# Loading the first experts' weights in half pieces beside the attention, on one Trainium2 core

## The chip, the cores and the metric

The kernel runs on one core of one Trainium2 chip. The time is the device time of one execution in microseconds (us). A kernel is executed several times, in turns with the kernel before on the same chip. An execution is called fast or slow by its time against the fastest of the same kernel, and ratios use fast executions alone. TensorE is written PE, its weight loads PEld, VectorE DVE, ScalarE ACT, GpSimd POOL and SyncE SP.

## The reference, cut to what matters

A recurrent attention (4 batches, 8 heads, 768 steps, head width 48) makes 3072 rows of 384. A router deals these rows out to 8 experts, 384 rows each, and each expert is two matrix products with a ReLU between.

```python
for t in range(S):                                      # attention, per batch and head
    cur = einsum(u * k[t], v[t])
    y[t] = einsum(r[t], state + cur)
    state = w[t][:, None] * state + einsum(k[t], v[t])
# x = the rows of y, 3072 x 384
logits = x @ w_gate                                     # 8 experts
order = argsort(-logits.flatten())                      # a row goes to its best expert that has room
...                                                     # (cut) cap = 384 rows for each expert
for e in range(8):
    out[mask_e] = maximum(x[mask_e] @ w1[e], 0) @ w2[e] # w1: 384 x 1024, w2: 1024 x 384
```

## The kernel before

The attention is cut into 24 units (6 pieces of 128 steps for each of 4 batches). Each unit needs four loads of 192 KB, of r, k, v and w, which SyncE issues on a hardware queue. Some units later come the logits; the routing starts on the first rows ("early") while the last units are still at work, so that the experts can begin soon after unit 23. A scheduler in the program orders all instructions by planned times; `op["G", 16]` below is unit 16's step G, the score products, and `after=[...]` makes an instruction follow others in the plan.

The experts' weights (768 KB as bf16 for each of w1 and w2) are loaded by GpSimd, because they are f32 in memory and become bf16 on the way. The first four experts have buffers of their own; the other four reuse the attention's buffers.

```python
def _weight_loads(nc, e, w1sb, w2sb, moe_w1, moe_w2):
    return [lambda: nc.gpsimd.dma_start(
                out=w1sb, in_=moe_w1[e].rearrange("(fc p) f -> p fc f", p=128)),
            lambda: nc.gpsimd.dma_start(
                out=w2sb, in_=moe_w2[e].rearrange("(fc p) d -> p fc d", p=128))]

LOADS = 16
# ... (cut) inside the planning of the whole program:
for e in range(E):
    users = []                                   # (cut) steps that must be over before reuse, e >= 4
    both = []
    for i, fn in enumerate(_weight_loads(nc, e, *weights[e], moe_w1, moe_w2)):
        by = [op["G", LOADS + 2 * len(loads)]] if len(loads) < 3 else []
        a = line.add("Wi", (e, i), "POOL", 800, fn, after=begun + users + by, prio=-0.9)
        begun = [a] if not loads else [a, loads[-1]]
        loads.append(line.add("Wd", (e, i), "DMA", 3500, lambda: None, after=[a],
                              lag=1900, prio=-0.3))
        both.append(loads[-1])
    loaded.append(both)
```

So the first three loads are planned beside units 16, 18 and 20, and every later one follows when the one before is planned to have landed. How far ahead the attention's own loads are issued is set by a table:

```python
PACE = {"Lw": [("G", 5)], "Lk": [("T1", 3)], "Lr": [("U", 3)], "Lv": [("T0", 1)]}
```

## Time and profile before

| | before |
|---|---|
| time, median of 3 executions | 253.95 us (252.87 to 258.76) |
| time of the execution that was profiled | 266.54 us, its span 264.6 us |
| PE busy in that span | 215.1 us (81%), mean granted clock 0.931 |
| DMA packets | 118388, mean 160 GB/s |
| weight loads | 16 of 768 KB, by GpSimd |
| attention loads | 96 of 192 KB, by SyncE |

The profiled execution took 12.6 us more than the median one. The prediction below shows the lines of this profile and reads them.

### The profile page before, as it was taken

Reading aid. Unit: us, or ns where it says so; the run is one execution under the profiler, and the core shown is the slowest. Engines: PE = TensorE matmul, PEld = TensorE weight load, DVE = VectorE, ACT = ScalarE, POOL = GpSimd, SP = SyncE. Lnnn points to the kernel's source line nnn. Section 1 sums busy time; section 2 is a strip of 40 time slices with the busy share of each in tenths; the row PEclk is TensorE's granted clock in tenths of the full one; section 3 lists DMA queues with packets and bytes.
Section 4 is the critical chain, followed back from the end, with each engine's and each line's share of the span. In section 5 each row is a group of like instructions: output and inputs, shape, how many; then the busy total and the mean of one; then the engine's idle time right before and its main releaser. Section 6 shows DMA issues by size and latency. Waiting matters only on the chain.

```text
span 264.6 us, 10437 instructions
## 1 busy us (share of the span) xinstructions
PE 215.1 (81%) x4469; PEld 160.1 (61%) x4469; DVE 142.9 (54%) x440; ACT 131.3 (50%) x248; POOL 148.6 (56%) x180
## 2 busy tenths in 40 slices
PE   2189998799999799789689491899899997959980
PEld 0166776577777587656477370777566765736850
DVE  6757667385677566557268760274755660114450
ACT  2156776485777577457344320374755663402300
POOL 7435685555766558747634548157764647563341
PEclk9999999999999999999779855699999999997995
DMA  7978789488879768999996993979999999231111
GB/s 149 183 148 165 143 168 223 92 173 194 160 152 214 143 131 172 193 197 168 177 228 95 206 175 80 180 165 221 167 198 213 201 191 266 86 112 67 59 69 62
DMA packets 118388, 42.24 MB, mean 160 GB/s; under 512 B 101440, under 2 KB 113728, under 8 KB 118336
## 3 DMA queue, kind: packets, MB, share of 16 engines
q1 hardware_dynamic: 104128, 21.84, 41.0%
q0 software_dynamic: 14208, 19.66, 38.3%
q8 instruction: 37, 0.61, 0.9%
q14 instruction: 15, 0.12, 0.2%
HBM read 46.61 MB, written 7.47 MB: 204 GB/s over the span
## 4 chain that ended last, share of the span: by engine, by line
PE 68%; DVE 8%; DMA 8%; issue 7%; another core or an unknown queue 3%; ACT 3%; POOL 2%; POOLq 0%; DVEq 0%
PE yps L320 11%; PE tps L478 8%; PE gps L320 7%; PE tps L320 7%; PE cps L320 7%; PE gps L1117 6%; PE gps L1148 6%; PE cps L1117 6%; PE cps L1148 5%; DMA vv<-in_moe_w_dram 4%; DMA ww<-in_w_dram 3%; PE tps L590 2%; PE tps L1087 1%; DVE Dohl L870 1%
## 5 line engine op out<-in xcount | busy, mean ns | idle before, releaser
L466 POOL TENSOR_TENSOR mm<-diag,dd 128x512 f32<-128x512 f32 x24 | 25.1, 1048 | 57.5 <-DVE dd L461 31.1
L484 ACT COPY krT<-tps 112x512 f32<-112x512 f32 x48 | 28.1, 586 | 23.4 <-PE tps L478 20.4
L1168 POOL DMA_INDIRECT out_dram<-Fos,tok x24 | 24.1, 1003 | 24.7 <-DVE Fos L1158 13.7
L1076 POOL DMA_INDIRECT Fxg<-x_scratch,tok x24 | 23.5, 977 | 20.3 <-PE tps L1087 11.1
L557 DVE COPY_PREDICATED mm<-mask,gps 128x256 f32<-128x256 uint8 x48 | 18.7, 442 | 27.9 <-PE gps L320 16.7
L320 PE MATMUL cps<-ww,negut 128*128 128x384 f32 x48 | 23.3, 569 | 12.1 <-issue 6.3
L478 PE MATMUL tps<-ident,krs 128*112 128x128 f32 x192 | 31.5, 290 | 0.6 <-DVE Dboth L710 0.6
L478 PEld LDWEIGHTS tps<-ident,krs 128*112 128x112 f32 x192 | 22.7, 140 | 10.9 <-issue 6.2
L320 PE MATMUL yps<-mm,vv 64*48 64x64 f32 x768 | 19.9, 232 | 9.0 <-DVE mm L557 6.0
L457 POOL TENSOR_TENSOR rku<-rku,u_bc 128x384 f32<-128x384 f32 x24 | 24.0, 1000 | 2.6 <-DMA u_bc<-in_u_dram 2.6
L453 POOL TENSOR_TENSOR rku<-kr 128x384 f32<-128x384 f32 x24 | 24.1, 1003 | 2.2 <-DMA kr<-in_r_dram 2.2
L320 PEld LDWEIGHTS yps<-mm,vv 64*48 64x48 f32 x768 | 14.6, 125 | 17.5 <-DVE mm L557 10.7
L1148 PEld LDWEIGHTS <-Fhs 128*128 128x128 bf16 x192 | 17.8, 99 | 11.9 <-issue 2.8
L578 ACT COPY xf<-yps 128x512 f32<-128x512 f32 x24 | 14.0, 582 | 22.1 <-PE yps L320 22.1
L447 DVE TENSOR_TENSOR krs<-kr,cps 128x768 f32<-128x768 f32 x24 | 22.7, 945 | 1.7 <-ACT cps L442 1.6
L320 PE MATMUL yps<-krT,sm 48*48 48x64 f32 x384 | 21.6, 229 | 1.1 <-issue 1.1
L442 ACT ACTIVATE cps<-cps 128x768 f32<-128x768 f32 x24 | 19.3, 804 | 5.0 <-DVE cps L438 5.0
L320 PE MATMUL yps<-krT,st 48*48 48x64 f32 x384 | 21.3, 228 | 0.3 <-issue 0.3
L1134 ACT ACTIVATE Fhs<-gps 128x512 bf16<-128x512 f32 x20 | 12.0, 598 | 15.5 <-PE gps L1117 9.4
L320 PE MATMUL gps<-krT 48*64 48x64 f32 x768 | 18.4, 227 | 1.0 <-issue 1.0
L1134 ACT ACTIVATE Fhs<-cps 128x512 bf16<-128x512 f32 x20 | 11.8, 598 | 13.8 <-PE cps L1117 10.3
L1117 PEld LDWEIGHTS <-w 128*128 128x128 bf16 x192 | 15.1, 100 | 5.8 <-issue 4.1
(200 smaller groups left out, 464.5 us busy)
## 6 DMA issues: line engine op xcount, KB each, us to landing
w<-in_moe_w_dram POOLq DMA_DIRECT2D x8, 768.0 KB
ww<-in_w_dram SPq DMA_DIRECT2D x24, 192.0 KB, 3.9
kr<-in_k_dram SPq DMA_DIRECT2D x24, 192.0 KB, 4.0
kr<-in_r_dram SPq DMA_DIRECT2D x24, 192.0 KB, 4.2
vv<-in_v_dram SPq DMA_DIRECT2D x24, 192.0 KB, 4.1
kr<-in_moe_w_dram POOLq DMA_DIRECT2D x4, 768.0 KB
x_scratch<-row SPq DMA_DIRECT2D x7, 384.0 KB, 4.9
vv<-in_moe_w_dram POOLq DMA_DIRECT2D x2, 768.0 KB
```

Source lines behind the costliest of these rows:

```text
L320: ln.last = nc.tensor.matmul(*a, **kw)
L447: fn=lambda u=u, kr=kr, b=b: nc.vector.tensor_tensor(out=KR[slot(("kr", u))][:, :, :, :D], in0=kr[:, b].rearrange("t x (h d) -> t x h d", ...
L453: fn=lambda u=u, kr=kr, b=b: nc.gpsimd.tensor_tensor(out=P[slot(("p", u))], in0=kr[:, b, 0, :], in1=kr[:, b, 1, :], op=ALU.mult))
L457: fn=lambda u=u: nc.gpsimd.tensor_tensor(out=P[slot(("p", u))], in0=P[slot(("p", u))], in1=u_bc, op=ALU.mult))
L466: fn=lambda u=u: nc.gpsimd.tensor_tensor(out=M[slot(("m", u))], in0=_free(diag, [0, 2], [0, NPAIR], [1, 64]), in1=_free(Dg[slot(("dg", u)) ...
L478: ln.last = nc.tensor.transpose(t[:112, at:at + 128], pair_of(s[:, x], j), ident)
L484: nc.scalar.copy(out=KRT[slot(("krt", u))][:112, 2 * half:2 * half + 2].rearrange("p j x t -> p (j x t)"), in_=Tps[slot(("t", u, half))][: ...
L1076: got = nc.gpsimd.indirect_dma_start(out=self.xg[slot[xg[1]]], out_offset=None, in_=self.x_dram, in_offset=bass.IndirectOffsetOnAxis(ap=to ...
L1117: nc.tensor.matmul(self.bank("B", b[1])[:, i * size:(i + 1) * size], lhsT=w1sb[:, k, f8 * 128:(f8 + 1) * 128], rhs=xv()[:, k], start=(k == ...
L1134: nc.scalar.activation(out=to, in_=of, func=AF.Relu)
L1148: nc.tensor.matmul(self.bank("B", b[1])[:, :DX], lhsT=hv()[:, f8, h * 128:(h + 1) * 128], rhs=w2sb[:, f8, :], start=(f8 == 0), stop=(f8 == ...
L1168: put = nc.gpsimd.indirect_dma_start(out=self.out, out_offset=bass.IndirectOffsetOnAxis(ap=tok[:, j:j + 1], axis=0), in_=self.os[slot[o[1] ...
```

## The change

The intent was to take the weight loads away from the last units of the attention, where the routing, the attention's own end and the hand-over to the experts meet. The loads of the first four experts are cut into 16 half pieces of 384 KB, planned one beside each of units 5 to 20. None stands beside units 21 to 23. The loads of the last four experts are halved too, and start behind the last unit.

```diff
-    return [lambda: nc.gpsimd.dma_start(
-                out=w1sb, in_=moe_w1[e].rearrange("(fc p) f -> p fc f", p=128)),
-            lambda: nc.gpsimd.dma_start(
-                out=w2sb, in_=moe_w2[e].rearrange("(fc p) d -> p fc d", p=128))]
+    w1 = moe_w1[e].rearrange("(fc p) f -> p fc f", p=128)
+    w2 = moe_w2[e].rearrange("(fc p) d -> p fc d", p=128)
+    f, k = F // 2, F // 256
+    return [lambda to=to, of=of: nc.gpsimd.dma_start(out=to, in_=of)
+            for to, of in ((w1sb[:, :, :f], w1[:, :, :f]), (w1sb[:, :, f:], w1[:, :, f:]),
+                           (w2sb[:, :k], w2[:, :k]), (w2sb[:, k:], w2[:, k:]))]
@@
-LOADS = 16
+LOADS = 5
@@
-                by = [op["G", LOADS + 2 * len(loads)]] if len(loads) < 3 else []
+                n = len(loads)
+                by = [op["G", LOADS + n if n < 4 * OWN else last]]
                 a = line.add("Wi", (e, i), "POOL", 800, fn, after=begun + users + by, prio=-0.9)
-                begun = [a] if not loads else [a, loads[-1]]
-                loads.append(line.add("Wd", (e, i), "DMA", 3500, lambda: None, after=[a],
+                begun = [a] if n < 4 * OWN else [a, loads[n - 2]]
+                loads.append(line.add("Wd", (e, i), "DMA", 1750, lambda: None, after=[a],
                                       lag=1900, prio=-0.3))
-                both.append(loads[-1])
+                both += [loads[-1]] * (i % 2)
```

## The prediction

> **What bounds the kernel now.** I read the page's forty slices first, then the busy table by stretches, then the chain that ended last in order of time, then the timelines of GpSimd and of TensorE around the gaps in it, and last the packets of the transfers. The stretches are: the quiet part of the attention (units 8 to 15), the last units with the weight loads beside them, the hand-over, and the experts.
>
> ```profile
> 60.00:100.00 40.00, 37.97 (x1123) 29.10 (x1126) 25.73 (x63) 26.73 (x52) 25.22 (x30) 1.00 0.81 166
> 112.00:130.00 18.00, 13.72 (x434) 10.42 (x425) 9.68 (x23) 10.63 (x20) 11.10 (x13) 0.98 1.04 186
> 130.00:140.00 10.00, 9.12 (x181) 6.70 (x181) 5.90 (x15) 4.30 (x10) 4.32 (x5) 0.70 0.99 187
> 140.00:158.00 18.00, 13.55 (x364) 10.94 (x363) 13.95 (x55) 6.39 (x12) 7.64 (x10) 0.77 1.01 167
> 158.00:171.00 13.00, 6.67 (x109) 4.84 (x107) 1.03 (x3) 2.25 (x6) 6.67 (x8) 0.53 0.66 124
> 171.00:208.00 37.00, 35.86 (x299) 25.66 (x300) 21.46 (x96) 21.68 (x43) 23.13 (x25) 1.00 1.00 197
> ```
>
> The columns are the stretch, its length, busy time of PE, PEld, DVE, ACT and POOL, the granted clock, the DMA share and GB/s. In the quiet part PE is busy 37.97 of 40 us and the DMA 0.81 of it: PE bounds, but the DMA has only a fifth left. From 112 to 158 the DMA is full, PE falls to 36.4 of 46 us, and the clock sinks. From 171 the experts keep PE at 97% again.
>
> The chain says what those gaps are:
>
> ```profile
> 118.97 1.05 SPq L333 DMA_DIRECT2D vv<-in_v_dram  x1
> ...
> 119.36 0.95 POOL L1026 DMA_DIRECT2D w<-in_moe_w_dram  x1
> ...
> 120.13 8.59 DMA ww<-in_w_dram
> 128.74 0.85 ACT ww L399
> 129.63 1.65 PE cps L320 x2
> ...
> 157.21 7.93 another core or an unknown queue
> ...
> 208.45 11.26 DMA vv<-in_moe_w_dram
> 219.76 1.48 PE gps L1117 x12
> ```
>
> A whole weight load (768 KB) is triggered at 119.36; the attention's own load of w, issued at 120.13, lands 8.59 us later where the median of these loads is 3.9, and the next matmul runs at half clock (1.65 us, against 0.71 in the quiet part). The second gap lies between the scores of the last unit and their use. The third is less than it looks: the timeline of PE shows it at work during most of those 11.26 us,
>
> ```profile
> 219.76 1.48 PE L1117 MATMUL gps<-Fxe,vv 128*128 128x256 bf16 x12 [1.65 <-DMA vv<-in_moe_w_dram]
> ```
>
> so that the late weights of the last expert cost 1.65 us.
>
> As a clock for the units I take the starts of their score matmuls (gps<-krT) in PE's timeline: unit 5 at 43.5, 16 at 104.2, 21 at 141.1, 23 at 157.4; the first expert matmul comes at 171.4. Units 5 to 16 take (104.2-43.5)/11 = 5.5 us each, units 16 to 23 take 53.2/7 = 7.6.
>
> **What the Trainium skill says.** "DMA: Bandwidth & Descriptors", section "Queues, rings and completion order": each of the 16 engines takes turns between its queues packet by packet. The trace agrees, to the loads' harm: in the packet records the attention's packets are 192 B and those of w1 2048 B, and while the first w1 load drains, 17 to 24 KB of the former go per 1.5 us beside 256 to 274 KB of the latter, some 8%, near 192/(192+2048). A drain of a whole load, about 5 us, is thus nearly a stop for the attention's loads. "Runtime: NRT & Kernel Launch", section "Instruction fetch mechanics": instructions come in 16 KiB blocks by the same DMA. The records show such blocks 4.6 us apart on average in the quiet part and 6 to 10 us apart around the five drains from 108 to 158: PE's waits marked "issue" belong to this. "TensorE: Matmul & The Clock Gate", section "What's actually happening": idle time of some microseconds halves the clock; the 0.53 from 158 to 171 agrees.
>
> **The change, part by part.** Bytes stay the same. Sixteen halves of 384 KB, planned beside units 5 to 20, replace eight whole loads, of which six are now triggered from 104.90 to 147.93 and two at 163.68 and 164.48, behind the first gathers. The other four experts' loads are halved too; they move ahead of where they are, since the first experts' loads are no longer in front of them. In the order of instructions, PE's list is unchanged up to the end of the last unit, where the first gathered rows now stand ahead of two small transposes; GpSimd gets its triggers between the attention's products, and none in the last units before the gathers.
>
> Removed, in times of this trace. (a) Units 16 to 23 take 53.2 us where 7 x 5.5 = 38.5 would be quiet; 14.7 over. Of this some 4 is the early routing, which stays (PE waited 3.46 us for VectorE at 151.2, with no load in it): 10.5 removed. (b) From the last scores to the first expert matmul are 14.0 us. Its own work, summed from the timeline's rows at full clock: scores 0.6, masks 0.8, products 1, two evictions 1.2, transposes 0.9, one wait for gather and eviction 2, is 6.5; 7.5 is removable. But the 7.93 of it is charged to an unknown queue, not to a weight transfer, and the profiled execution (266.5 us) is itself 12.5 over the median timed one, so it may not be there in timed runs. I count 5. (c) The wait for the last expert's weights: 1.65. Sum 17.
>
> Added. (d) DMA work per unit from the fastest rates in the packet records: 4096 packets of 192 B at 1600 per 1.5 us are 3.84 us; a quarter of a 384 KB store is 0.45; half a weight load is 384 packets of w1 at 156 per 1.5 us halved, 1.85, or 512 of w2 at 400 per 1.5 us, 1.92. Sum 6.2 us, against the 5.5 the unit takes now: the DMA becomes the bound of units 5 to 20. 16 x (6.2-5.5) = 11. (e) Triggers: whole ones take 818 and 944 ns; eight more before and eight more after the hand-over, at some 0.85 us, are 7 us of GpSimd each time. A unit occupies it 1.00+1.00+1.05+0.5 = 3.6 us of 5.5, and in the experts it is busy 23.1 of 37 us, so this fits beside: 0.
>
> Net 17-11 = 6 us, 2.4% of 254: 248.
>
> **The rivals.** First, the spread costs more than it removes. For it: where both kinds of transfer were in flight the DMA moved 186 GB/s at a share of 1; a unit with half a load needs 786+98+393 = 1277 KB, so 6.9 us at that rate, and 16 x 1.4 = 22 us are added instead of 11; then the time is 259. Against it: that rate includes stalls of the issuing queues behind a whole load, and the experts' stretch reaches 197 to 218 GB/s. Second, the halves disappear in the idle fifth of the DMA: a half stops the attention's loads for only 2 us, less than the slack of most of them (k, r and v are issued several us before use; only w has about 1). Then (d) is 3 to 4 us and the time is 240. Third, the end does not move because it hangs on the routing: the first gather waits for the early routing, which follows unit 19's logits by a long chain on VectorE. In the trace the row numbers are ready at 156.0, only 1.3 us before the last scores; if units 20 to 23 speed up, this chain takes the wait's place. It caps (a)+(b) at perhaps 10 and makes 251 to 254. A fourth, that the experts wait for weights 4 to 7, I think unlikely: their triggers come some 12 us earlier.
>
> **Range and chances.** The middle of the working is 248; the second rival reaches 240, the first and third 251 to 259. I take 241 to 255 for 8 in 10. Gain over 2% means below 248.9, just above the middle: 0.52. Within 2% 0.39. Slower than 259 needs the first rival in full: 0.09.
>
> **What would show it.** Right: the chain no longer holds a wait of 8 us for ww; the DMA share from unit 5 to 20 is 0.95 or more instead of 0.81, and those units take 6.0 to 6.4 us each; unit 23's scores start between 150 and 160, the first expert matmul 6 to 8 us later; PE has no wait for vv in the experts; the granted clock stays at 1.00 through 130 to 140. Wrong: units 5 to 20 take near 5.5 us (second rival) or near 7 (first); or PE stands before the first gathered rows' transposes for more than 4 us (third).

## The result, and the profile after

The changed kernel is slower: 266.12 us median of 4 executions (264.63 to 270.07), against 254.27 us for the kernel before on the same chip (4 executions, 252.87 to 258.76). The ratio is 1.0465 with a 95% interval of 1.0354 to 1.0577. Here and below a ratio is the mean time of one kernel's fast runs over that of the other's fast runs of the same rounds, so it is not quite the ratio of the medians quoted. Time and direction both lie outside the prediction.

The profiled execution of the changed kernel took 267.36 us, a typical one for it. The profiled execution of the kernel before was not typical, so I profiled that kernel again (E0 below: 253.04 us, span 251.1 us), and compare with that profile. Its line numbers are one higher, because a comment line stands on top.

The unit clock of the prediction (starts of the score products in PE's timeline) then says where the time went:

| stretch | kernel before, re-profiled | changed kernel | difference |
|---|---|---|---|
| start to unit 5 | 44.9 | 43.2 | -1.7 |
| unit 5 to unit 16 | 59.6 | 75.4 | +15.8 |
| unit 16 to unit 23 | 53.6 | 52.3 | -1.3 |
| last scores to first expert product | 7.7 | 7.9 | +0.2 |
| experts, to PE's last end | 77.5 | 77.3 | -0.2 |
| after PE's last end | 7.8 | 9.3 | +1.5 |
| sum (span) | 251.1 | 265.4 | +14.3 |

All of the loss is in units 5 to 16, which had been quiet; the relieved units 16 to 23 gave back 1.3 us, and the hand-over and the experts nothing. The busy table by stretches shows both. First the kernel before; the columns are the stretch, its length, the busy time of PE, PEld, DVE, ACT and POOL, the granted clock, the DMA share and GB/s:

```profile
44.90:104.50 59.60, 56.04 (x1722) 43.27 (x1716) 38.62 (x94) 41.42 (x79) 37.67 (x45) 1.00 0.82 167
104.50:158.10 53.60, 43.30 (x1140) 33.05 (x1135) 34.26 (x102) 24.73 (x47) 29.34 (x34) 0.84 1.01 178
```

The same stretches of the changed kernel, then its last units alone, then its experts:

```profile
43.20:118.60 75.40, 62.69 (x1732) 47.38 (x1727) 39.00 (x95) 41.81 (x79) 47.39 (x57) 0.92 1.06 185
118.60:170.90 52.30, 41.83 (x1131) 32.25 (x1127) 34.15 (x101) 24.29 (x47) 26.06 (x30) 0.86 0.70 132
155.00:171.00 16.00, 11.96 (x341) 9.65 (x337) 12.56 (x51) 6.01 (x12) 4.54 (x5) 0.82 0.15 40
178.80:256.10 77.30, 76.66 (x722) 56.41 (x720) 38.99 (x156) 39.47 (x76) 51.86 (x57) 0.98 0.80 167
```

The same PE work (1722 and 1732 instructions) occupies PE for 62.69 us instead of 56.04, at a clock of 0.92 instead of 1.00. PE is idle for 12.7 us of the stretch instead of 3.6. The DMA, whose share is 1.06 here, stands nearly empty at 0.15 from 155 to 171, just where the change kept it free, and those units are no faster for it. And in the experts PE is at work for 76.66 of 77.30 us, so their weights are there in time.

What PE waited for from unit 5 to unit 16, in the kernel before (columns: waiter, released by what, us in total, times, longest):

```profile
PE tps L321 <- ACT krT L485: 1.4, 1, 1.4
PE gps L321 <- issue: 0.8, 1, 0.8
PE yps L321 <- issue: 0.8, 2, 0.4
PE tps L321 <- issue: 0.3, 1, 0.3
```

and in the changed kernel:

```profile
PE gps L320 <- DMA vv<-in_v_dram: 3.4, 2, 2.3
PE tps L320 <- issue: 2.6, 2, 1.6
PE gps L320 <- issue: 2.1, 3, 0.8
PE cps L320 <- ACT ww L399: 1.9, 1, 1.9
PE yps L320 <- issue: 1.9, 4, 0.7
PE tps L320 <- ACT krT L484: 0.6, 1, 0.6
```

This splits the 15.8 us. PE's busy time grew by 62.69 - 56.04 = 6.65 us. Waits for the attention's loads of v and w are new: 3.4 + 1.9 = 5.3 us (ACT's ww at L399 works on the loaded w). "Issue", in which PE waits for nothing that the profile shows, grew from 1.9 to 6.6 us, by 4.7. The wait for ACT's krT fell by 0.8. The sum is 15.85.

What "issue" is, the packet records tell. Instructions come in blocks of 16 KB on a DMA queue of their own, q8. While the attention runs (40 to 155 us, all 13 profiles), PE has 105 gaps of 0.25 us or more marked "issue", and every one ends 1.1 to 1.6 us after such a block has landed; of its 54 other gaps, 9 do. So these are waits for instructions. From unit 5 to unit 16 they come to 1.1 to 5.0 us in the seven profiles with no weight bytes there, or hardly any, and to 3.9 to 7.4 us in the six with them: late blocks are a second form of the delay, though 4.7 us is its size against E0 alone.

The lower clock has a plain place too. It is 0.50 in two spells: from 73.1 to 79.9 us, just after an "issue" wait of 1.64 us, and from 114.1 to 120.9 us, amid the waits for v and w. A wait for instructions is enough for such a spell: one of 1.99 us precedes a spell of 6.8 us in the profile of E2, where no weight load is near. It is not a rule, since the prediction's profile has a wait of 1.99 us too, at 47.7 us, and keeps its clock.

The chain that ended last in the changed kernel (start, length, what) has the stall that the change was to remove, once in this stretch and once more behind it:

```profile
99.54 6.52 DMA vv<-in_v_dram
...
107.48 7.28 DMA ww<-in_w_dram
114.79 0.85 ACT ww L399
115.68 1.65 PE cps L320 x2
...
134.28 7.85 DMA ww<-in_w_dram
142.15 0.85 ACT ww L399
143.04 1.65 PE cps L320 x2
```

As before, the products behind such a wait run at half clock (1.65 us for the pair that takes 0.71 elsewhere in this chain). GpSimd's timeline has half loads triggered at 106.38, 109.63 and 113.35, so a load of w issued at 107.48 travels beside two or three of them.

The DMA's queues from unit 5 to unit 16 (packets, MB, share of 16 engines; q0 carries the weights, q1 the attention's loads and stores), in the kernel before:

```profile
q1 hardware_dynamic: 47120, 9.71, 79.9%
```

and in the changed kernel:

```profile
q1 hardware_dynamic: 44488, 9.00, 61.6%
q0 software_dynamic: 5529, 4.69, 43.2%
```

Per unit, the attention's own packets take 79.9% x 59.6 / 11 = 4.33 us of all 16 engines before and 61.6% x 75.4 / 11 = 4.22 us after. Twelve half loads take 43.2% x 75.4 / 12 = 2.71 us each. The shares of the two queues sum to over 100%, so packet times overlap in part and are no measure of how full the DMA is. Nor do packets take longer in company: those of 768 and 1024 B take 86 and 112 ns here, and 86 and 108 ns in the experts, where no attention load is beside them.

### The profile page after: what moved, and what is told of

Same layout as the page of the kernel before. It is cut to its first block, busy times and chain, and to the rows that moved or that the text cites. A ratio compares the mean times of both kernels' runs of the same rounds, so it can differ in the third digit from the quotient of the medians.

```text
span 265.4 us, 10455 instructions
## 1 busy us (share of the span) xinstructions
PE 218.0 (82%) x4469; PEld 163.3 (62%) x4469; DVE 143.3 (54%) x440; ACT 131.5 (50%) x248; POOL 159.6 (60%) x196
## 4 chain that ended last, share of the span: by engine, by line
PE 65%; DMA 10%; issue 7%; DVE 7%; POOL 4%; ACT 2%; SPq 2%; POOLq 0%; DVEq 0%
PE yps L320 10%; PE tps L320 7%; PE tps L478 7%; PE gps L320 6%; PE cps L1150 6%; PE cps L1119 6%; PE gps L1119 6%; DMA ww<-in_w_dram 6%; PE gps L1150 6%; PE cps L320 5%; DMA vv<-in_v_dram 2%; PE tps L590 2%; DMA u_bc<-in_u_dram 2%; SPq L333 2%; PE tps L1089 1%
## 5 line engine op out<-in xcount | busy, mean ns | idle before, releaser
L320 PE MATMUL cps<-ww,negut 128*128 128x384 f32 x48 | 24.8, 602 | 14.8 <-issue 5.5
L478 PE MATMUL tps<-ident,krs 128*112 128x128 f32 x192 | 32.2, 295 | 1.4 <-ACT row L604 0.8
L320 PE MATMUL yps<-krT,st 48*48 48x64 f32 x384 | 22.4, 234 | 0.6 <-issue 0.6
L320 PE MATMUL yps<-krT,sm 48*48 48x64 f32 x384 | 22.3, 235 | 0.6 <-issue 0.6
L578 ACT COPY xf<-yps 128x512 f32<-128x512 f32 x24 | 13.9, 580 | 16.7 <-PE yps L320 16.6
L438 DVE SCALAR_TENSOR_TENSOR cps<-cps,ww 128x384 f32<-128x384 f32 x24 | 13.6, 565 | 11.8 <-PE cps L320 10.5
L320 PE MATMUL gps<-vv,krs 64*48 64x48 f32 x768 | 14.6, 214 | 6.0 <-DMA vv<-in_v_dram 3.4
L320 PEld LDWEIGHTS yps<-krT,sm 48*48 48x48 f32 x384 | 15.7, 130 | 5.5 <-issue 4.5
L320 PE MATMUL gps<-krT 48*64 48x64 f32 x768 | 17.7, 232 | 1.3 <-issue 1.3
```

Of the source, the lines that this page charges most:

```text
L320: ln.last = nc.tensor.matmul(*a, **kw)
L478: ln.last = nc.tensor.transpose(t[:112, at:at + 128], pair_of(s[:, x], j), ident)
```

## The experiments

Three theories stood at first. A, throughput: the DMA has become the bound of units 5 to 20, since early bytes fill its idle rest and the overflow costs time. B, taking turns: each early load delays the attention's loads, whatever idle rest there is, so that each costs its share even when they are few. C, the halving itself costs: smaller packets and more triggers. The letters in the texts stand for these. E0 to E3 ran on one chip, and E4 to E8 on the same chip (medians of the kernel before 255.28 and 255.22 us). E9 to E11 ran on a slower chip.

### E0: the kernel before, profiled again

The edit is a comment line.

> The kernel before, profiled again. Its first profiled execution was 266.5 us, 12 over its timed median of 254. If that execution was an unlucky one, this profile should come out near 254, with the wait of 7.9 us after the last scores and the trickle of matmuls at 233 to 238 us gone or much shorter, and the last expert matmul some 77 to 80 us after the first (as in the changed kernel). If profiling itself costs 12 us, it comes out near 266 again.

It took 253.04 us (one execution, span 251.1). Unit 23's scores start at 158.1, and the first expert product at 165.84, 7.7 us later, where the profile of the prediction had 14.0. The chain of this hand-over holds no long wait; the longest is one of 1.05 us:

```profile
159.75 1.05 issue
160.80 0.83 PE yps L321 x39
...
162.03 2.22 PE tps L321 x32
```

The experts take 77.5 us, where the prediction's profile had 85.3. So the stall of 7.93 us charged to an unknown queue, and a slow stretch in the experts, are not in a usual execution on this chip, and part (b) of the prediction's gain was not there to be taken. On the slower chip both come back (E9, E10).

### E1: whole loads, as early

```diff
# in the kernel before
-by = [op["G", LOADS + 2 * len(loads)]] if len(loads) < 3 else []
+by = [op["G", 5 + 2 * len(loads) if len(loads) < 8 else last]]
-begun = [a] if not loads else [a, loads[-1]]
+begun = [a] if len(loads) < 8 else [a, loads[-1]]
```

> Whole loads, one beside every second unit from the sixth on: as early and as many bytes per unit as the change, not halved. Theory A (throughput: the DMA carries too many bytes in units 5 to 20, whatever the pieces): 262 to 268 us, units 5 to 21 near 6.8 us each, perhaps a little better than the change because the 2048 B packets of w1 stay whole. Theory B (collisions: what counts is how long one load stops the attention's loads): worse than the change, 268 to 280. Theory C (the halving itself, smaller packets and twice the triggers, is the cost): near 250 to 256.

The result was 269.92 us (267.26 to 272.65), ratio 1.0668 (1.049 to 1.0846). Units 5 to 16:

```profile
44.50:120.50 76.00, 61.86 (x1727) 46.60 (x1720) 38.69 (x94) 41.81 (x79) 44.45 (x52) 0.93 1.01 184
```

They take 76.0 us, against 75.4 for the halves: the same bytes at the same place cost the same, whole or halved. Units 16 to 23 take 57.4 us against 52.3, so for those the halves were the better form. The loss is due to the place, not to the cut. By the total, theory A's range is missed by 2 us and B's just met; the two were not yet told apart.

### E2: half loads, as late as before

```diff
# in the changed kernel
-by = [op["G", LOADS + n if n < 4 * OWN else last]]
+by = [op["G", 16 + n]] if n < 6 else []
-begun = [a] if n < 4 * OWN else [a, loads[n - 2]]
+begun = [a] if n < 2 else [a, loads[n - 2]]
```

> Halves, but at about the places where the kernel before has its whole loads (from the seventeenth unit on, the later ones behind the first gathers). Theory A: 250 to 257, as before, since no more bytes fall in units 5 to 20. Theory B: faster than before, 246 to 252, since each stop is half as long. Theory C: 260 or more.

The result was 256.69 us (253.24 to 258.45), ratio 1.011 (0.9938 to 1.0281). Halving without moving costs somewhere between nothing and 2.8%, and by the middle a quarter of the loss. It isn't the main cause, and theory C falls as such. So does what B expected of shorter stops, 246 to 252 us; A's range holds the result. The profile fell on a slow execution (258.45 us), and gives a measure of how far one profile can stray: units 5 to 16, with no weight load beside them, took 64.7 us at a clock of 0.92, 5 us more than in E0. The 75.2 to 76.0 us of the changed kernel, E1 and E6 are well beyond that.

### E3: the changed kernel with an eighth of the early bytes

```diff
# in the changed kernel, for the first four experts only (wrong on purpose)
-(w1sb[:, :, :f], w1[:, :, :f]), (w1sb[:, :, f:], w1[:, :, f:]),
-(w2sb[:, :k], w2[:, :k]), (w2sb[:, k:], w2[:, k:])
+(w1sb[:, :, :64], w1[:, :, :64]), (w1sb[:, :, f:f + 64], w1[:, :, f:f + 64]),
+(w2sb[:, :k, :64], w2[:, :k, :64]), (w2sb[:, k:, :64], w2[:, k:, :64])
+# and the weight buffers zeroed at the start
```

> The change's triggers at the change's places, each moving an eighth of the bytes for the first four experts (the rest of these weights is zero, so the result is wrong on purpose; the zeros are written at the start on VectorE and delay it by some us). Theory A and B: units 5 to 21 back to 5.3 to 5.7 us each. Theory C, in the form that the triggers on GpSimd cost: they stay near 7. In total: removing 16 x 1.4 us from 266 leaves 243 to 248, plus the delay of the start.

Triggers, their number and their places are those of the changed kernel; the w1 pieces move an eighth of their bytes, those of w2 a sixth. The packets stay nearly as many (4975 instead of 5529 on q0 in units 5 to 16); it is their size that falls. The output is wrong (relative error 0.698). The result was 256.28 us (254.73 to 258.27), ratio 1.0187 (1.0045 to 1.033), with the zeroing delaying unit 5 to 52.2, some 7.3 us later than in E0. Units 5 to 16 and 16 to 23:

```profile
52.20:111.10 58.90, 56.04 (x1724) 43.32 (x1719) 38.62 (x94) 41.20 (x79) 45.49 (x55) 1.00 0.99 174
111.10:161.90 50.80, 42.97 (x1137) 33.35 (x1130) 34.39 (x102) 24.53 (x47) 27.95 (x33) 0.86 0.56 105
```

With the bytes gone, the 15.8 us are gone: 58.9 us, 0.7 less than in the kernel before, at a clock of 1.00. The triggers on GpSimd cost nothing, as part (e) had it. Two more things are in these lines. The DMA share is 0.99 though nothing is slowed, so a share near 1 is not by itself a full DMA. And units 16 to 23 still take 50.8 us with hardly a weight byte beside them: by this pair of profiles late loads had cost the kernel before 53.6 - 50.8 = 2.8 us, not 10.5. That is a small difference between single profiles: this stretch takes 48.3 us in E8, with weights beside it, and 57.4 in E1.

### E4: a half load beside every other unit

```diff
# in the changed kernel
-by = [op["G", LOADS + n if n < 4 * OWN else last]]
+by = [op["G", 5 + 2 * n if n < 8 else 12 + n]] if n < 12 else []
-begun = [a] if n < 4 * OWN else [a, loads[n - 2]]
+begun = [a] if n < 12 else [a, loads[n - 2]]
```

> Halves of the first two experts beside every second unit from the sixth on (half the change's dose), four halves beside units 20 to 23, where the attention's own loads have run out, the rest as in the kernel before. Theory A (the bound is the DMA's throughput, and a unit has an idle rest of about 1 us of it): the dose needs 4.3 + 1.35 = 5.7 us of DMA per unit, so units 5 to 16 take 5.5 to 5.8 us instead of 6.85 and 5.4 without loads; in total 250 to 256, about the kernel before. Theory B (every piece costs by the load it stops, whatever rest there is): half of the change's loss, units 5 to 16 at 6.1 us, 258 to 261.

The result was 262.78 us (259.3 to 266.49), ratio 1.0289 (1.02 to 1.0379). The profile fell on an execution called slow (266.49 us). Units 5 to 16:

```profile
45.50:112.90 67.40, 58.89 (x1728) 45.16 (x1722) 38.99 (x94) 41.56 (x79) 42.13 (x50) 0.97 0.96 178
```

Six early halves cost 67.4 - 59.6 = 7.8 us, 1.3 each, where twelve had cost 15.8, 1.3 each. An idle rest that swallows the first ones would have shown here: from the packet times above, 4.33 + 6/11 x 2.71 = 5.8 us of DMA per unit, and the units took 6.13. So an idle rest of 0.18 in the DMA was not free room for other loads, and theory A alone is too small; B's number for the units fits. Two things weaken this. A slow execution can be 5 us longer in these units by itself (E2). And of the total, which lies above both ranges, 5.0 us fall in the experts (82.5 us instead of 77.5), so it does not decide.

B's mechanism, a load that is stopped and comes late, is not what PE shows in this stretch:

```profile
PE gps L320 <- issue: 5.1, 4, 1.6
PE yps L320 <- issue: 1.6, 2, 1.2
PE tps L320 <- ACT krT L484: 0.9, 1, 0.9
PE tps L320 <- issue: 0.7, 1, 0.7
```

No wait for a load is left, and 7.4 us are waits for instructions. At half the dose it was the instructions, and the clock after such waits, that made the units longer.

### E5: whole loads, three units later than before

```diff
# in the kernel before
-LOADS = 16
+LOADS = 19
-by = [op["G", LOADS + 2 * len(loads)]] if len(loads) < 3 else []
+by = [op["G", LOADS + 2 * len(loads)]] if len(loads) < 2 else []
```

> The kernel before with the first weight load at unit 19 instead of 16, so that nearly all weights fall into the time after the attention's last load. If the end slots are free: from unit 5 to 23 110 to 111 us instead of 113.5, but fewer weights are there at the start of the experts, which then wait: experts 79 to 85 us instead of 77.5; total 252 to 260. If the loads at 16 to 19 were what cost most before, it gains 2 to 4 us.

The result was 257.14 us (253.74 to 259.45), ratio 1.008 (0.998 to 1.018). In the profile, which fell on a slow execution, units 5 to 23 take 110.7 us against 113.2 in E0, but the experts 85.1 us against 77.5, with waits for weights in them. What later loads free beside the attention is given back in the experts; neither place is better beyond the noise, and later loads don't gain.

### E6: w1 cut by rows, so that packets stay at 2048 B

```diff
# in the changed kernel
-(w1sb[:, :, :f], w1[:, :, :f]), (w1sb[:, :, f:], w1[:, :, f:]),
+(w1sb[:, :1], w1[:, :1]), (w1sb[:, 1:], w1[:, 1:]),
```

> The change with w1 cut along its rows (one third and two thirds) instead of its columns, so that its packets keep 2048 B. Theory A with packet size in it: the w1 packets of the change took 42.8 us of 16 engines against 38.2 before, so this gives back up to 4.6 us in all, of which half falls in units 5 to 20: 262 to 265 us. If packet size is nothing: 265 to 267. If packet size is the main cost of the change (theory C): 254 to 258.

The result was 264.88 us (261.01 to 267.74), ratio 1.0342 (1.0218 to 1.0467), while the changed kernel had 1.0465. The intervals overlap. Units 5 to 16 take 6.83 us each (75.2 in all), where the changed kernel's take 6.85. So packet size explains nothing of the loss there. The middles of the two ratios are some 3 us apart, which the intervals leave open, and the total lies between the ranges for some effect and for none.

### E8: eight halves early, eight beside the last four units

```diff
# in the changed kernel
-by = [op["G", LOADS + n if n < 4 * OWN else last]]
+by = [op["G", LOADS + n if n < 8 else 16 + n // 2 if n < 4 * OWN else last]]
```

> The change for the first two experts (a half beside each of units 5 to 12), and the other eight halves two by two beside units 20 to 23. Theory A: units 5 to 13 near 6.9 us, units 13 to 20 back at 5.4 to 5.8, the last four units no slower than in the change; eight units of 1.4 us too many are left: 254 to 260 us. If the halves at the end hold up the first gathers: first expert matmul 10 us or more after the last scores instead of 7.7.

The result was 258.24 us (255.31 to 263.07), ratio 1.0066 (0.9968 to 1.0165). Its profile is of a fast execution; units 5 to 16 and 16 to 23:

```profile
43.40:111.30 67.90, 60.99 (x1729) 45.91 (x1722) 38.92 (x95) 41.63 (x79) 44.05 (x53) 0.95 1.03 191
111.30:159.60 48.30, 41.50 (x1135) 32.26 (x1129) 34.65 (x101) 24.39 (x47) 28.54 (x34) 0.87 0.83 155
```

Eight halves cost 8.3 us, 1.0 each. Units 5 to 13, each with its half, take 6.25 us, where 6.9 was expected; units 13 to 20 are back at 5.6. The other eight halves, planned two by two beside units 20 to 23, cost nothing that can be seen (by GpSimd's timeline six come in this stretch and two at 165.9, behind the last scores): units 16 to 23 take 48.3 us, 5.3 fewer than in E0, and the experts 77.5, the same. By the timeline of the kernel before (E0), SyncE issues the attention's last two loads from 137 to 142 us; from there on weights have the DMA nearly to themselves. That is the stretch which the change left empty. Still E8 does not beat the kernel before.

### E9 and E10: the attention's loads issued two units earlier

```diff
# E9: in the changed kernel; E10: in the kernel before
-PACE = {"Lw": [("G", 5)], "Lk": [("T1", 3)], "Lr": [("U", 3)], "Lv": [("T0", 1)]}
+PACE = {"Lw": [("G", 7)], "Lk": [("T1", 5)], "Lr": [("U", 5)], "Lv": [("T0", 3)]}
# and the planned times of these loads 9000 ns earlier
```

These ask whether the early loads cost time because the attention's loads land too late, which a longer lead would cure. On this chip the kernel before took 270.68 us (266.33 to 272.57, 11 executions).

> The change, with the attention's own loads paced two units further ahead of their use (same bytes, same weight triggers). Theory A' (the DMA cannot carry the bytes of a unit and its half in less than some 6.8 us, so no head start helps for long): units 5 to 16 stay at 6.5 to 6.9 us, total 262 to 267. Theory B' (latency: a half stops the attention's loads for 2 to 3 us and a load that is due within that time comes too late, so the cost lies in the short head start): units 5 to 16 fall to 5.5 to 6.0 us, total 248 to 256.

> The kernel before with the same wider pacing, as the control of the run beside it. Quiet units were bound by TensorE and its instructions, so 5.3 to 5.5 us there under both theories; under B' the units beside the whole loads gain up to 3 us, total 250 to 254; under A' nothing changes, 253 to 257.

E9 took 281.0 us (279.95 to 286.06), ratio 1.0442 (1.0327 to 1.0557). E10 took 269.78 us (268.01 to 270.97), ratio 1.0049 (0.997 to 1.0127). Units 5 to 16 of E9:

```profile
42.70:117.30 74.60, 63.10 (x1728) 48.14 (x1720) 38.75 (x94) 41.39 (x79) 48.00 (x58) 0.91 1.05 186
```

and of E10:

```profile
43.20:106.90 63.70, 59.48 (x1725) 46.13 (x1720) 38.62 (x94) 41.54 (x79) 36.89 (x44) 0.95 0.86 175
```

What PE waited for in this stretch of E9:

```profile
PE gps L320 <- issue: 5.0, 4, 2.4
PE gps L320 <- DVE sp L517: 4.3, 2, 4.1
PE tps L320 <- issue: 1.1, 2, 0.8
PE yps L320 <- issue: 0.8, 1, 0.8
```

PE's direct waits for loads are gone from the list, 5.3 us of them in the changed kernel, and the stretch is still 10.9 us longer than in E10. "Issue", the waits for instructions, is 6.9 us against 1.3 in E10; the wait for VectorE's sp is 4.3 against 2.5 (VectorE itself had just waited 5.1 us for a store of finished rows, 3.5 in E10); PE's busy time is 3.6 us longer. A lead that is too short is thus not the cause alone: it was one form in which the delay showed, and late instructions are another, which a longer lead of the loads does not touch. With a longer lead the loss may be smaller (10.9 us here, 15.8 on the other chip), but the total's ratio is no better than the changed kernel's.

The hand-over of E10 has the stall of the prediction's profile again:

```profile
160.80 7.80 another core or an unknown queue
```

Its experts take 84.4 us. E9 has the stall too (7.75 us, and 13.9 us from the last scores to the first expert product, as in E10). So it is seen in three profiles, two of them typical executions on the slower chip, and in no profile of E0 to E8 or of the changed kernel; the change does not remove it. In all three VectorE's masking of the last scores waits about 8 us for something that the profile does not name. What that is stays open.

### E11: routing begun after the last unit

```diff
# in the kernel before
-first = deal.early(tok1, a1, op["LF", EARLY - 1], zero, *built)
+first = deal.early(tok1, a1, op["LF", EARLY - 1], op["MS1", last], zero, *built)
```

> The kernel before with the early routing begun only after the last unit's scores are used, to see what makes units 16 to 23 slow (53.6 us; 50.8 with hardly any weight bytes). If it is the routing's work between the units: 41 to 46 us for units 16 to 23, with the weight loads still beside them, and a hand-over longer by some 15 us. If it is the weight loads after all: 50 us or more.

One execution took 272.58 us. Units 16 to 23:

```profile
106.90:152.70 45.80, 37.75 (x1083) 29.18 (x1076) 21.99 (x52) 23.87 (x46) 26.75 (x32) 0.89 0.90 166
```

They take 45.8 us, against 54.1 in E10 on the same chip (with the wider pacing) and 53.6 in E0. VectorE's work there falls from 34.26 us (E0) to 21.99, and PE's waits for the routing's tiles, 5.2 us in E0, are gone. The hand-over grows to 29.7 us from 13.9 in E10, so nothing is gained in total. In the kernel before the last units were thus slow mainly for the routing on VectorE, some 8 us by this one execution, and for a smaller part for the weights (2.8 us by E3). Two of the six whole loads come only in the last microsecond here, so a part of the 8 us may be theirs.

## Why the prediction was wrong

**The end that the change was to free.** Part (a) counted 10.5 us removable in units 16 to 23 and part (b) 5 us in the hand-over. Both were mis-sized. For (a), the working allowed the routing 4 us, the one visible wait for VectorE, and charged the rest to the weights (14.7 - 4 is 10.7, by the way); E11 gives the routing some 8 us, and E3 leaves 2.8 for the weights, each from one profile. The changed kernel got 1.3. For (b), the prediction said that the wait "may not be there in timed runs" and still counted 5; E0 shows 0 (7.7 us before, 7.9 after). The wait of part (c) did go (1.3 us in E0, none after), but PE's busy time in the experts grew by 1.1 us, and they take 77.5 us in E0 and 77.3 after. So 17 us of gain were 1 or 2.

**The cost beside the quiet units.** Part (d) is the step that failed and decided the sign. It took the DMA's own work, 6.2 us, for the length of a unit, so that only what goes over the 5.5 us is paid: 0.7 us. The units took 6.85 us (75.4 / 11) against 5.42 in E0, 1.4 us more, double the cost. The work itself was not far off: the attention's part is 3.84 + 0.45 = 4.29 us expected, 4.33 and 4.22 in packet time, and by the prediction's rates the packets that went in these units (42759 of 192 B, two stores of 384 KB, twelve halves) are some 66 us of work in 75.4 us (an estimate). What failed is the overlap: PE did not keep pace with the DMA, but waited for loads and for instructions and then ran at half clock. E4 shows the same at half the dose, where (d)'s rule gives 4.3 + 6/11 x 1.9 = 5.3 us of work, less than the 5.5 of the unit, and so no cost; 1.3 us for each half were paid (in a slow execution).

**What the cost consists of.** The working looked on the DMA alone. It had itself said that PE's waits marked "issue" belong to the instruction blocks, which is right, and then gave them no cost: they grew by 4.7 us. It also left out that a PE which waits can slow down: 6.65 of the 15.8 us are the same PE work at a lower clock, more than the 5.3 us of waits for loads themselves.

**The rivals.** The first rival was the right one in its numbers: 1277 KB at 186 GB/s, 6.9 us per unit. The trace has 185 GB/s and 6.85 us. It said 259 because it still took off the gain of 17 us, and because it charged 1.4 us to sixteen units, where only the eleven from 5 to 16 had been quiet. 254 + 11 x 1.4 - 1.5 = 268 is near the 266 measured. The argument against it, that its rate "includes stalls of the issuing queues behind a whole load", was the mistake: the halves made the same loss (E1: 76.0 us whole, 75.4 halved). The second rival, the idle fifth, falls with the result itself, and with E8 and E4. The third, that PE would stand before the first gathered rows, is not seen (7.9 us in the hand-over), though by E11 its routing chain is what mostly keeps units 16 to 23 slow.

**The signs named beforehand.** Right were the first expert product 6 to 8 us behind the last scores (7.9), no wait for weights in the experts, a DMA share over 0.95 (1.06), and unit times near 7 as the sign of the first rival. The clock was 1.00 from 130 to 140, as written, but by luck: half-clock spells lie before it (114.1 to 120.9) and behind it (141.4 to 148.2), and the mean was 0.92 in units 5 to 16 and 0.86 in units 16 to 23. Wrong were the chain without 8 us for w (7.28 and 7.85), units of 6.0 to 6.4 us, and unit 23 between 150 and 160 (170.9).

**What is shown and what stays open.** It is shown that the bytes of the early loads cause the loss (E3), about 1.0 to 1.4 us for each half load against E0 (E8, E4, E1), that the triggers (E3) do not, that the cut (E1, E2) and packet size (E6) are not the main cause, and that a longer lead of the attention's loads does not cure it (E9). A single profile can stray: units 5 to 16 took 58.9 to 64.7 us in the seven profiles with no weight bytes there, or hardly any, and 67.4 to 76.0 in the six with them. That PE's loss takes three forms, late loads, late instruction blocks and the lower clock, is read from the traces. How the delay divides between the throughput of the DMA and the turns that its queues take is not settled.

## What to carry to other kernels

A stretch in which the DMA seems to have a fifth to spare is no free room when the engine beside it lives on small loads with a short lead and gets its instructions by the same DMA: put large loads where the other queue has stopped, even if that place looks crowded on other engines. Take the rate for a mixed stretch from a stretch that is already mixed, not from the best rates of each kind alone (here 6.9 us against 6.2, for 6.85 measured), and add what late instructions and a lower clock cost. Before counting a stall as gain, see that the profiled execution is as long as the timed ones, and ask which engine would keep the stretch slow without it.

## What the Trainium skill lacked or had wrong

- "DMA: Bandwidth & Descriptors", section "Queues, rings and completion order", tells of turns between queues, but not what a GpSimd load costs the loads of a hardware queue beside it. Here each 384 KB half lengthened the attention by 1.0 to 1.4 us (E8, E4, E1). The page counts a packet as some 9 to 17 descriptors; whether the profile's records of 192 and 2048 B are packets in that sense no run shows, so the 8% in the prediction agrees with turns one by one, but does not prove them.
- "TensorE: Matmul & The Clock Gate", section "What's actually happening", puts the ramp penalty under 1% of a typical kernel's span. Here the same PE work took 62.69 us instead of 56.04 in one stretch at a clock of 0.92, and those 6.65 us are 2.5% of the span of 265.4. The figure is no guide for a kernel like this, in which the half clock came back in two spells of 6.8 us.
- "Runtime: NRT & Kernel Launch", section "Instruction fetch mechanics", calls the cost of crossing a block mostly hidden. PE's "issue" waits in units 5 to 16, which end 1.1 to 1.6 us after a block has landed, were 1.9 us of 59.6 in E0, and 6.6 us of 75.4 beside weight loads. There the fetch was not hidden.
- No page that I read gives the spread between chips: the same kernel had a median of 255.22 us on one chip and 270.68 us on another, 11 executions each.
